# A state-space scan with a gated feed-forward on one core: pairs 3 to 11 turned by one transposing DMA a pair, all wide decays in one prologue set, and SP's and GpSimd's work for pairs 2 to 6 reordered

## The chip, the core and the metric

The kernel runs on one NeuronCore of a Trainium2 chip. The core has a matrix engine (TensorE, PE in the profile), a vector engine (VectorE, DVE), a scalar engine (ScalarE, ACT), GpSimd (POOL), a queue engine that only issues DMAs here (SyncE, SP), and 16 DMA engines that all queues share. The metric is the device time of one execution in microseconds; lower is better.

## The reference

For each of 4 batches and 8 heads, a scan over 768 positions in chunks, with head size 32 and state size 16, and then a feed-forward layer over the 3072 tokens (the heads side by side make 256 features):

```python
cum = np.cumsum(la, axis=-1)                      # la: log of a, in a chunk
L = np.exp(cum[..., :, None] - cum[..., None, :]) * causal
M = einsum('bhin,bhjn->bhij', Cc, Bc) * L
y = einsum('bhij,bhjd->bhid', M, xc) \
    + einsum('bhin,bhnd->bhid', Cc, state) * exp(cum)
state = exp(sum(la)) * state + sum_j(Bc x xc * exp(cum[-1] - cum))
...
out = (relu(x @ w_gate) * (x @ w_val)) @ w_out    # 256 -> 1536 -> 256
```

## The kernel before

**Tiling.** The scan works in chunks of 128 positions, two at a time: a pair is 256 tokens of one batch, three pairs a batch (PPB), twelve pairs in all (NPAIR). The feed-forward works in blocks of 512 tokens, two pairs each, six blocks (NBLK). The decay is not applied to the score matrix: B is divided by the running product of `a`, and C is multiplied by it, after which the scores need only a causal mask.

**What is done for a pair.** `load...` brings x, B and C from memory. `scale_bc` multiplies B and C by their decays and makes them bf16, with token positions on the partitions and the 8 heads x 16 states (128) along the row. `cast_x` makes x bf16. Then B and C must be turned, so that heads x states lie on the partitions: `transp`/`turn` do this with TensorE transposes into PSUM, and `tevac` copies the results out, B twice, each time with half of the heads set to zero (`BT`), and C once (`CT`). `G` forms the scores of the 8 heads: 16 products with a contraction over 32 partitions (two heads, of which one is zeroed). `gevac` brings them to bf16 with the causal mask: on VectorE by a product with `maskUT`, on ScalarE by a plain copy that GpSimd masks behind it (`causal`). `Dm` multiplies them by x, `inter` adds C times the carried state, and `yevac` copies the sum, transposed, to `yT`, which is the feed-forward's input. `astep` adds B^T x of a chunk to the state in PSUM (`A_ps`), and `sevac` copies the blocks of it that belong to one head each.

**Three layouts.** Pairs 0 to 3 (`p < NWIDE`) are loaded wide: partition p holds tokens 2p and 2p+1, so that a memory run is 128 bytes. Their B and C get their decays from small fp32 products of their own (`wide_decay`, `wide_factors`, in the sets [1] and [2, 3]), and B is sorted back to the order of the tokens for `astep` by four products with a permutation (`sort_b`, `sort_evac`). Pairs 4 and 5 are loaded with one token on a partition and turned by TensorE. For pairs 6 to 11 (`p >= NRUN`, batches 2 and 3) B and C are loaded a second time, a whole batch at once, with runs of 24 positions on a partition (`load_seq`); VectorE scans the decays in that layout (`seq_scan` to `seq_mids`), GpSimd scales (`seq_scale`), VectorE turns 32x32 blocks (`seq_turn`) and sorts and masks the words (`seq_part`). Their states come from `arun`, in `A_ps`' bank.

**The feed-forward.** `gv` makes one slice of 128 hidden features for 512 tokens, `gvp` two slices for 256 tokens; ScalarE takes the relu (L715, L742), VectorE the product (L719, L749). `outs` makes 128 output rows.

**Order.** Every engine's instructions run in the order in which the program is written (`in_order`). The order is laid out by hand at the end of the kernel (L830 to L1008) and from block 2 on by a loop (L1010): the feed-forward of a block, with `scale` of the next pairs in between, then `section(P, Q)`, which finishes pair P and forms the scores of Q, then `outs`. PSUM has one bank for `A_ps` and seven (`bank`) that are used in turn. DMAs of the loads and most stores are issued by SP in the order of the program, the weights by GpSimd.

Of the kernel before, what the change touches and what calls it, by code (L numbers as in the profile page):

```python
# [8 lines left out]
FP32 = mybir.dt.float32  # L9
# [20 lines left out]
def kernel(  # L30
# [41 lines left out]
    NWIDE = 4  # L72
# [25 lines left out]
    def load(p, q):  # L98
        b, c0 = p // PPB, 2 * (p % PPB)
        if p >= NRUN:  # L100
            xr = raw.tile([128, 2, NH, D], FP32, tag="xr", name="xr")
            br = raw.tile([128, 2, NH, N], FP32, tag="br", name="br")
            for i in range(2):
                sl = slice((c0 + i) * 128, (c0 + i + 1) * 128)
                q.dma_start(out=xr[:, i], in_=x[b, :, sl, :].rearrange("h s d -> s h d"))
                q.dma_start(out=br[:, i], in_=B[b, :, sl, :].rearrange("h s n -> s h n"))
            st[p] = {"xr": xr, "br": br}
            return
        xr = raw.tile([128, 2, NH, D], FP32, tag="xr", name="xr")
        bcr = raw.tile([128, 2, 2, NH, N], FP32, tag="bcr", name="bcr")  # L110
        for i in range(2):
            sl = slice((c0 + i) * 128, (c0 + i + 1) * 128)
            q.dma_start(out=xr[:, i], in_=x[b, :, sl, :].rearrange("h s d -> s h d"))
            for src, j in ((B, 0), (C, 1)):
                q.dma_start(out=bcr[:, i, j],
                            in_=src[b, :, sl, :].rearrange("h s n -> s h n"))
        st[p] = {"xr": xr, "bcr": bcr}

    U = S // 32
    B0 = NRUN // PPB  # L120
    NSEG = 2 * (NB - B0)
    seq = {}

    def load_seq(b, q):

        s = {}
        for src, k in ((B, "B"), (C, "C")):
            r = raw.tile([128, 2, U, N], FP32, tag="seq" + k, name="seq" + k, bufs=2)
            q.dma_start(
                out=r.rearrange("p t u n -> p t (u n)"),  # L130
                in_=src[b].rearrange("(t q) (j u) n -> (q j) t (u n)", t=2, u=U))
            s[k] = r
        seq[b] = s
# [32 lines left out]
    smasks = const.tile([128, 2, 2, 128], BF16)  # L166
    pick = const.tile([2 * BH, 2, BH], FP32)
    pairs = identf.rearrange("p (h w) -> p w h", w=2)
    nc.vector.tensor_copy(pick[:, 1], pairs[:, 1])
    sel = const.tile([2 * BH, 128], FP32)  # L170
# [51 lines left out]
    def wide_decay(ps, d=None):  # L222

        if d is None:
            d = bank("wdec", (128, len(ps), 2, 8))
        first = True
        for k, p in enumerate(ps):
            b, c0 = p // PPB, 2 * (p % PPB)
            for i in range(2):
                w, o = (c0 + i) // HC, ((c0 + i) % HC) * 128  # L230
                for r in range(2):
                    nc.tensor.matmul(  # L232
                        out=d[64 * i:64 * i + 64, k, r],
                        lhsT=cp[:, o + r:o + 128:2], rhs=pick[:, w, 8 * b:8 * b + 8],
                        start=first or (k == 0 and r == 0), stop=True,
                        tile_position=(0, 64 * i), skip_group_check=True)
                first = False
        return d
# [27 lines left out]
    def wide_factors(ps, d):  # L266
        f = const.tile([128, len(ps), 2, 2, 8], FP32, name="wf%d" % ps[0])
        nc.vector.reciprocal(f[:, :, 0], d)
        nc.vector.tensor_copy(f[:, :, 1], d)
        for k, p in enumerate(ps):  # L270
            factors[p] = f[:, k].rearrange("p j r h -> p (j r) h")

    scaleBC = glob.tile([128, NB, NC, 2, 8], FP32)
# [12 lines left out]
    def decay_evac(d):  # L286
        for w in range(2):
            cs = slice(w * HC, (w + 1) * HC)
            nc.scalar.copy(
                out=scaleBC[:, :, cs, 1, :].rearrange("p b k h -> p k b h"), in_=d[:, :, w])  # L290

    def inverse(b, c0, c1):
        nc.vector.reciprocal(scaleBC[:, b, c0:c1, 0, :], scaleBC[:, b, c0:c1, 1, :])

    ah = const.tile([128, NSEG, U], FP32)
    a0 = const.tile([128, NSEG, U], FP32)
    hd = const.tile([128, 2, NSEG, U], FP32)
    tot = const.tile([128, 32], FP32)
    tott = const.tile([128, 32], FP32)
    lead = const.tile([128, 2, 17], FP32)  # L300
    half = const.tile([128, 1], FP32)
    mids = const.tile([128, 32], FP32)
    pre = const.tile([128, 32], FP32)

    def load_a(q):
        q.dma_start(out=ah, in_=a[B0:NB].rearrange("b (t q) (j u) -> (q j) (b t) u", t=2, u=U))

    def seq_start():
        for v in (a0, tot, lead):
            nc.gpsimd.memset(v, 0.0 if v is a0 else 1.0)  # L310
        nc.gpsimd.memset(smasks, 0.0)
        nc.gpsimd.tensor_copy(a0[:, :, 0], ah[:, :, 0])
        nc.gpsimd.memset(ah[:, :, 0], 0.0)

    def seq_masks():
        nc.gpsimd.tensor_scalar_mul(words, tmask, -1.0)
        for q in range(4):
            r = slice(32 * q, 32 * q + 32)
            for v in range(2):
                nc.gpsimd.tensor_copy(  # L320
                    smasks[r, v, :, 32 * q:32 * q + 32],
                    tmask[r].unsqueeze(2).to_broadcast([32, 2, 32]))

    def seq_scan():
        local = hd[:, 1]
        nc.vector.tensor_tensor_scan(
            out=local.rearrange("p k u -> p (k u)"), data0=ah.rearrange("p k u -> p (k u)"),
            data1=a0.rearrange("p k u -> p (k u)"), initial=0.0, op0=ALU.mult, op1=ALU.add)

    def seq_totals():  # L330
        nc.vector.tensor_copy(tot[:, 0:NSEG], hd[:, 1, :, U - 1])
        nc.vector.transpose(out=tott, in_=tot)

    def seq_lead():
        for k in range(2):
            nc.vector.tensor_tensor_scan(
                out=lead[:, k, 1:17], data0=tott[:, 16 * k:16 * k + 16],
                data1=zero.to_broadcast([128, 16]), initial=1.0, op0=ALU.mult, op1=ALU.add)
        nc.vector.reciprocal(half, lead[:, 0, 16:17])

    def seq_mids():
        nc.vector.tensor_scalar_mul(mids[:, 0:16], lead[:, 0, 0:16], half)
        nc.vector.tensor_copy(mids[:, 16:32], lead[:, 1, 0:16])
        nc.vector.transpose(out=pre, in_=mids)

    def seq_decay():
        local = hd[:, 1]
        nc.gpsimd.tensor_tensor(
            out=local, in0=local, in1=pre[:, 0:NSEG].unsqueeze(2).to_broadcast([128, NSEG, U]),
            op=ALU.mult)  # L350

    def seq_inverse(b):
        r = slice(2 * (b - B0), 2 * (b - B0) + 2)
        nc.vector.reciprocal(hd[:, 0, r], hd[:, 1, r])

    U32 = mybir.dt.uint32
    V = U // 2
# [130 lines left out]
    def tevac(p, beng, ceng):  # L488
# [20 lines left out]
        if not wide:  # L509
            c_copy()  # L510
# [564 lines left out]
```

## Time and profile before

| | us |
|---|---|
| median of 3 runs (lowest, highest) | 125.64 (125.1, 126.44) |
| the profiled execution | 124.8 |
| its span, first to last instruction | 123.0 |
| TensorE busy | 118.3 |
| VectorE busy | 92.1 |
| ScalarE busy | 74.6 |
| GpSimd busy | 49.7 |

In the rows of the timeline, the first column is the start from the beginning of the span, the second how long the instruction or the run of equal instructions lasted, then the engine, the line, the operation, what it writes and reads, the shapes and the count. In brackets stands how long the engine was idle before it and what ended that. A name with q (SPq) is an engine's queue, for DMA issues. In the row of a wait the numbers are the total, the number of times and the longest. A "group" row gives the busy time of all its instructions and the mean of one in ns. How long a DMA takes from its issue to its landing is given as lowest, median and highest.

### The profile page before, as it was taken

Reading aid. Unit: us, or ns where it says so; the run is one execution under the profiler, and the core shown is the slowest. Engines: PE = TensorE matmul, PEld = TensorE weight load, DVE = VectorE, ACT = ScalarE, POOL = GpSimd, SP = SyncE. Lnnn points to the kernel's source line nnn. Section 1 sums busy time; section 2 is a strip of 40 time slices with the busy share of each in tenths; the row PEclk is TensorE's granted clock in tenths of the full one; section 3 lists DMA queues with packets and bytes.
Section 4 is the critical chain, followed back from the end, with each engine's and each line's share of the span. In section 5 each row is a group of like instructions: output and inputs, shape, how many; then the busy total and the mean of one; then the engine's idle time right before and its main releaser. Section 6 shows DMA issues by size and latency. Waiting matters only on the chain.

```text
span 123.0 us, 3313 instructions
## 1 busy us (share of the span) xinstructions
PE 118.3 (96%) x1251; PEld 81.1 (66%) x1257; DVE 92.1 (75%) x196; ACT 74.6 (61%) x148; POOL 49.7 (40%) x102
## 2 busy tenths in 40 slices
PE   6999999999999999999999999999999999999990
PEld 4678795578888989744478644588544587444780
DVE  2786898889999859879995889981898770678420
ACT  4376668888764461767663776746676644767310
POOL 7989741885745676477330640030700030000000
PEclk9999999999999999999999999999999999999999
DMA  2999999999989979969921282003200003100022
GB/s 61 201 193 209 168 167 190 130 102 174 162 101 278 140 137 191 199 201 211 132 24 62 83 137 22 5 0 106 70 3 0 0 5 128 43 0 0 0 91 85
DMA packets 63568, 12.95 MB, mean 105 GB/s; under 512 B 55168, under 2 KB 63552, under 8 KB 63552
## 3 DMA queue, kind: packets, MB, share of 16 engines
q1 hardware_dynamic: 54160, 9.47, 42.9%
q0 software_dynamic: 4272, 2.36, 14.6%
q10 hardware_dynamic: 5120, 0.90, 3.9%
q8 instruction: 10, 0.16, 0.5%
q14 instruction: 6, 0.05, 0.1%
HBM read 11.94 MB, written 3.15 MB: 123 GB/s over the span
## 4 chain that ended last, share of the span: by engine, by line
PE 95%; DVE 1%; issue 0%; ACTq 0%; ACT 0%; DVEq 0%
PE o L760 25%; PE val L707 20%; PE gate L704 18%; PE gate L734 7%; PE val L734 6%; PE w L189 4%; PE y L670 3%; PE g L544 3%; PE y L660 2%; PE A_ps L586 1%; PE tp L486 1%; PE wdec L232 1%; PE dec L279 1%; PE o L796 1%; PE bp L463 1%; PE fdec L247 0%
## 5 line engine op out<-in xcount | busy, mean ns | idle before, releaser
L719 DVE TENSOR_TENSOR h<-r,val 128x512 bf16<-128x512 bf16 x54 | 35.9, 685 | 10.2 <-ACT r L715 9.6
L715 ACT ACTIVATE r<-gate 128x512 bf16<-128x512 f32 x54 | 32.2, 598 | 12.2 <-PE gate L704 11.7
L707 PE MATMUL val<-yT,wv 128*128 128x512 bf16 x108 | 32.1, 379 | 0.3
L760 PE MATMUL o<-wo,h 128*128 128x256 bf16 x276 | 32.3, 273 | 0.0
L704 PE MATMUL gate<-yT,wg 128*128 128x512 bf16 x102 | 30.8, 379 | 0.0
L552 POOL TENSOR_SCALAR_AFFINE_SELECT gs<-gs 128x512 bf16<-128x512 bf16 (+1 forms) x26 | 13.6, 547 | 41.6 <-ACT gs L569 41.6
L760 PEld LDWEIGHTS <-h 128*128 128x128 bf16 x276 | 26.2, 98 | 4.0
L576 DVE TENSOR_TENSOR gs<-g,maskUT 128x512 bf16<-128x512 f32 (+1 forms) x32 | 17.6, 601 | 7.1 <-PE g L544 4.0
L707 PEld LDWEIGHTS <-wv 128*128 128x128 bf16 x108 | 10.6, 98 | 12.7
L704 PEld LDWEIGHTS <-wg 128*128 128x128 bf16 x108 | 10.4, 98 | 11.1
L569 ACT CAST gs<-g 128x512 bf16<-128x512 f32 (+1 forms) x26 | 11.8, 512 | 2.9 <-PE g L544 2.9
L742 ACT ACTIVATE r<-gate 128x512 bf16<-128x512 f32 x18 | 10.6, 604 | 2.7 <-PE gate L734 2.3
L749 DVE TENSOR_TENSOR h<-r,val 128x512 bf16<-128x512 bf16 x18 | 11.8, 678 | 0.3 <-ACT r L742 0.2
L734 PE MATMUL gate<-yT,wg 128*128 128x256 bf16 x72 | 10.8, 273 | 0.0
L734 PE MATMUL val<-yT,wv 128*128 128x256 bf16 x72 | 10.8, 273 | 0.0
L779 ACT COPY ob<-o 128x512 f32<-128x512 f32 x6 | 3.5, 586 | 8.6 <-PE o L760 8.6
L774 ACT COPY ob<-o 128x256 f32<-128x256 f32 x10 | 3.7, 373 | 7.3 <-PE o L760 6.8
L734 PEld LDWEIGHTS <-wv 128*128 128x128 bf16 x72 | 7.0, 98 | 0.9
L692 ACT CAST yT<-y 128x512 bf16<-128x512 f32 x10 | 5.9, 586 | 2.4 <-PE y L670 2.3
L734 PEld LDWEIGHTS <-wg 128*128 128x128 bf16 x72 | 6.7, 98 | 0.9
L189 PE MATMUL w<-warm 128*128 128x256 bf16 x27 | 5.9, 380 | 1.2 <-DVE tmask L159 1.2
L452 POOL CAST xb<-xr 128x512 bf16<-128x512 f32 x10 | 6.1, 612 | 1.0 <-DMA xr<-in_x_dram 1.0
(124 smaller groups left out, 123.2 us busy)
## 6 DMA issues: line engine op xcount, KB each, us to landing
xr<-in_x_dram SPq DMA_DIRECT2D x24, 128.0 KB, 3.7
out_dram<-ob SPq DMA_DIRECT2D x6, 256.0 KB, 2.6
out_dram<-ob SPq DMA_DIRECT2D x9, 128.0 KB, 1.8
wo<-in_moe_w_out_dram POOLq DMA_DIRECT2D x1, 768.0 KB, 8.9
seqB<-in_B_dram SPq DMA_DIRECT2D x2, 384.0 KB, 3.7
seqC<-in_C_dram SPq DMA_DIRECT2D x2, 384.0 KB, 4.2
br<-in_B_dram SPq DMA_DIRECT2D x12, 64.0 KB, 3.2
wg<-in_moe_w_gate_dram POOLq DMA_DIRECT2D x3, 128.0 KB, 4.3
```

The lines of the kernel that those rows point to most:

```text
L189: nc.tensor.matmul(out=w[:, 0:cols], lhsT=warm[:, 0:128], rhs=warm[:, 0:cols], start=True, stop=True)
L552: nc.gpsimd.affine_select(out=dst, in_=dst, pattern=[[0, n], [1, 128]], compare_op=ALU.is_ge, fill=0.0, base=0, channel_multiplier=-1)
L569: nc.scalar.copy(out=d[:, q, h], in_=g[q][:, h])
L576: nc.vector.tensor_tensor(out=d[:, q, h], in0=g[q][:, h], in1=m[:, h], op=ALU.mult)
L704: nc.tensor.matmul(out=g, lhsT=wg[:, k, fs], rhs=yT[:, k, tk], start=(k == 0), stop=(k == 1))
L707: nc.tensor.matmul(out=v, lhsT=wv[:, k, fs], rhs=yT[:, k, tk], start=(k == 0), stop=(k == 1))
L715: nc.scalar.activation(r, g, AF.Relu)
L719: nc.vector.tensor_tensor(out=fst[b][:, f], in0=r, in1=v, op=ALU.mult)
L734: nc.tensor.matmul(out=o[:, j], lhsT=w[:, k, fs], rhs=yT[:, k, tk], start=(k == 0), stop=(k == 1), skip_group_check=True)
L742: nc.scalar.activation(r, g, AF.Relu)
L749: nc.vector.tensor_tensor(out=fst[b][:, f:f + 2, u * 256:(u + 1) * 256], in0=r, in1=v, op=ALU.mult)
L760: nc.tensor.matmul(out=o[:, ts % 2], lhsT=fst[b][:, f, ts * 128:(ts + 1) * 128], rhs=wo[:, f], start=(f == 0), stop=(f == NF - 1), skip_gr ...
```

## The change

NWIDE is 3 instead of 4. The layouts of pairs 3, of pairs 4 and 5, and of pairs 6 to 11 give way to one:

- `load_bc` loads C wide (two tokens a partition) and B narrow (one).
- `scale_bc` writes into one of four bf16 tiles `pads` of 128 x 6 x 128: for each of the two chunks, B's even and odd heads into two blocks whose other columns stay zero (`diag`), and C into the last two. From pair 6 on it writes B, dense, a second time (`bt`), for `arun`.
- `dturn` turns all six blocks with one transposing DMA from SP, from SBUF to SBUF.
- `G` and `inter` read the result as it lies; the scores' columns then stand with even tokens first, so that the masks (`maskW`, and `causal` with a wide pattern), the y bank and `yevac` follow that order. `astep` for pairs 3 to 5 becomes two products of 128 columns, one for the even heads and one for the odd.
- `wide_decay` makes the decays of all pairs in one set, in the prologue, where five warming products and the set [1] stood; C of all pairs reads its copy `wD`. The decays of single tokens (`decay`) are now for B alone (`cN`, and `iN`, their inverse).
- The functions `load_seq` and all `seq_...` go, with their masks.
- In the hand-written part the loads, scalings, casts and turns of pairs 2 to 6 are put in another order.

```diff
-    NWIDE = 4
+    NWIDE = 3
...
+    def load_bc(p, q=nc.sync, hold=False):
...
+        q.dma_start(out=cr.rearrange("p h r n -> p h (r n)"),
+                    in_=C[b, :, sl, :].rearrange("h (p r) n -> p h (r n)", r=2))
         for i in range(2):
             sl = slice((c0 + i) * 128, (c0 + i + 1) * 128)
+            q.dma_start(out=br[:, i], in_=B[b, :, sl, :].rearrange("h s n -> s h n"))
+    def load(p):
+        load_bc(p)
+        load_x(p)
...
+    pads = [glob.tile([128, 6, 128], BF16, name="pad%d" % k) for k in range(NPAD)]
+    for k in range(2, 4):
+        nc.vector.memset(pads[k][:, 0:4], 0.0)
...
+    def wide_decay():
+        d = bank("wdec", (128, PPB, 2, BH))
+        for c in range(0, NC, 2):
+            for r in range(2):
+                for i in range(2):
+                    w, o = (c + i) // HC, ((c + i) % HC) * 128
                     nc.tensor.matmul(
+                        out=d[64 * i:64 * i + 64, c // 2, r],
+                        lhsT=cp[:, o + r:o + 128:2], rhs=pick[:, w],
...
+        if p >= NWIDE:
+            s["pad"] = t = pads[p % NPAD]
+            for i in range(2):
                 eng.tensor_tensor(
+                    out=diag(t, 2 * i), in0=s["br"][:, i].rearrange("s (q t) n -> s q t n", t=2),
+                    in1=iN[:, i, p].rearrange("s (q t) -> s q t", t=2).to_broadcast(
+                        [128, 4, 2, N]), op=ALU.mult)
+            eng.tensor_tensor(
+                out=t[:, 4:6].rearrange("s r (h n) -> s r h n", n=N),
+                in0=s["cr"].rearrange("s h r n -> s r h n"),
+                in1=wD[:, p % PPB, :, 8 * b:8 * b + 8].to_broadcast([128, 2, NH, N]), op=ALU.mult)
+            if p >= NRUN:
+                bt = att.tile([128, 2, 128], BF16, tag="bt", name="bt")
...
+    def dturn(p):
+        s = st[p]
+        s["TT"] = att.tile([128, 6, 128], BF16, tag="TT", name="TT")
+        nc.sync.dma_start_transpose(out=s["TT"], in_=s["pad"].rearrange("s k m -> s (k m)"))
...
+            for t in range(2):
+                nc.tensor.matmul(
+                    out=heads[:, :, t], lhsT=st[p]["pad"][:, 2 * i + t], rhs=own[:, :, t],
+                    start=(c == 0 and t == 0), stop=(c == NC - 2), skip_group_check=True)
...
     astep(0, 0)
-    keep_warm(5)
-    d1 = wide_decay([1])
-    wide_factors([1], d1)
+    dw = wide_decay()
+    wide_factors(dw)
     load_wide(2, nc.sync, True)
-    load_x(2)
     sevac(0, 0)
     scale_bc(1, nc.gpsimd)
     dall = decay()
-    decay_evac(dall)
+    nc.scalar.copy(out=wD, in_=dw)
     split_y(0)
+    decay_evac(dall, 0)
+    load_x(2)
+    load_bc(3)
...
     astep(1, 1)
-    d2 = wide_decay([2, 3], later)
-    wide_factors([2, 3], d2)
     gvp_mul(*u4)
-    load_wide(3, nc.sync, True)
+    inverse(NWIDE, 6)
+    scale_bc(2, nc.gpsimd)
     load_x(3)
-    load(4, nc.sync)
-    load(5, nc.sync)
-    load_seq(2, nc.sync)
-    load(6, nc.sync)
-    scale(2, nc.gpsimd, nc.gpsimd)
+    cast_x(2, nc.gpsimd)
+    for k in range(2):
+        nc.gpsimd.memset(pads[k][:, 0:4], 0.0)
+    scale_bc(3, nc.gpsimd)
+    dturn(3)
+    load_bc(4)
+    load_bc(5)
     sevac(1, 1)
...
-    turn(3, True)
-    sort_b(3, False)
-    tevac(3, nc.vector, nc.scalar)
     gvp(1, 0, 0)
...
     gvp_evac(*u)
-    seq_masks()
-    scale(4, nc.gpsimd, nc.gpsimd)
+    scale_bc(4, nc.gpsimd)
+    dturn(4)
+    load_x(4)
+    load_x(5)
+    load_bc(6)
+    cast_x(4, nc.gpsimd)
     gvp(1, 0, 6)
...
     scale(5, nc.gpsimd, nc.gpsimd)
-    turn(4)
-    tevac(4, nc.vector, nc.scalar)
+    dturn(5)
+    load_x(6)
     gvp(1, 1, 10)
     outs(0, 0)
     state(4, 0)
     Gs(4)
+    scale_bc(6, nc.gpsimd)
     outs(0, 1)
     state(4, 1)
+    dturn(6)
+    load(7)
     outs(0, 2)
-    turn(5)
-    tevac(5, nc.vector, nc.scalar)
     outs(0, 3)
-    load(8, nc.sync)
+    load(8)
     section(4, 5)
-    scale(6, nc.gpsimd, nc.gpsimd)
+    cast_x(6, nc.gpsimd)
...
     for b in range(2, NBLK):
+        if more:
+            scale(Q, nc.gpsimd, nc.gpsimd)
+        if P + 3 < NPAIR:
+            load(P + 3)
+        if more:
+            dturn(Q)
...
             if f == 4 and R < NPAIR:
                 scale(R, nc.gpsimd, nc.gpsimd)
+                dturn(R)
```

More of the change, by code (lines that the diff above doesn't have):

```diff
@@ L284, in decay @@
         return d
[L286 to L357, printed above, removed]
-    packs = [glob.tile([128, V, 32, 2], BF16, name="pack%d" % k) for k in range(4)]
-    words = const.tile([128, 2], mybir.dt.int32)
@@ L569, in gevac @@
             nc.scalar.copy(out=d[:, q, h], in_=g[q][:, h])
-            causal(d[:, q, h], 2 * n)
+            causal(d[:, q, h], 2 * n, p >= NWIDE)
         for q in range(3, -1, -1):
@@ L835 @@
     first_scale(0, fB, bs0[:, 0:2])
+    load_x(1, True)
     first_scale(1, dC, bs0[:, 2:4])
@@ L896 @@
     gvp_mul(*u0)
-    later = bank("wdec", (128, 2, 2, 8))
     u2 = gvp(0, 0, 2, False)
```

288 lines of the change are left out of this document (98 added, 190 removed).

## The prediction

> **What bounds the kernel now.** I read the busy shares and the chain of waits first, then TensorE's own waits, then the timeline of TensorE against those of GpSimd, SP and ScalarE around pairs 1 to 6.
>
> ```profile
> span 123.0 us, 3313 instructions
> ## 1 busy us (share of the span) xinstructions
> PE 118.3 (96%) x1251; PEld 81.1 (66%) x1257; DVE 92.1 (75%) x196; ACT 74.6 (61%) x148; POOL 49.7 (40%) x102
> ```
>
> ```profile
> PE 95%; DVE 1%; issue 0%; ACTq 0%; ACT 0%; DVEq 0%
> ```
>
> ```profile
> PE w L189 <- DVE tmask L159: 1.2, 1, 1.2
> ```
>
> The chain that ends last is TensorE for 95% of the span, and TensorE's only recorded wait is the 1.2 us before its first warming matmul. From there it goes from one product to the next. So what the change takes from VectorE (the 32x32 turns and word masks of pairs 6 to 11, the masked copies of the turned B of pairs 3 to 5) gains nothing by itself. Only two things move the end: matmuls taken out of TensorE's queue, and operands that now arrive too late for it. I work out both in turn. The profiled execution took 124.8 us, 1.8 over its span, and that 1.8 stays. The median of the runs shown is 125.64, 0.84 above it.
>
> **What leaves TensorE.** Pair 3 loses its four transposes and the four products that sort its B:
>
> ```profile
> 25.41 0.27 PE L486 MATMUL tp<-ident,bs 128*128 128x128 bf16 x2
> 25.53 0.28 PE L486 MATMUL tpc<-ident,bs 128*128 128x128 bf16 x2
> 25.64 0.39 PE L463 MATMUL bp<-bs,order 128*128 128x128 bf16 x4
> 25.86 0.60 PE L734 MATMUL gate<-yT,wg 128*128 128x256 bf16 x4
> ```
>
> From the start of the first to the start of the gate product is 25.86 - 25.41 = 0.45 us. (The second column is longer, because matmuls overlap; I go by starts throughout.) Pairs 4 and 5 lose four transposes each:
>
> ```profile
> 36.79 0.39 PE L486 MATMUL tp<-ident,bs 128*128 128x128 bf16 x4
> 37.01 0.60 PE L734 MATMUL gate<-yT,wg 128*128 128x256 bf16 x4
> ```
>
> ```profile
> 42.48 0.39 PE L486 MATMUL tp<-ident,bs 128*128 128x128 bf16 x4
> 42.70 1.47 PE L760 MATMUL o<-wo,h 128*128 128x256 bf16 x12
> ```
>
> That is 0.22 twice, 0.44. The wide decays of pairs 2 and 3 go from behind pair 1 into the prologue:
>
> ```profile
> 15.13 0.27 PE L586 MATMUL A_ps<-xb,bx 128*128 128x256 bf16 x1
> 15.33 0.68 PE L232 MATMUL wdec<-pick,cp 64*64 64x8 f32 x16
> 15.94 0.61 PE L734 MATMUL gate<-yT,wg 128*128 128x256 bf16 x4
> ```
>
> ```profile
> 15.33 0.37 ACT L651 CAST yT<-y 128x256 bf16<-128x256 f32 x1 [0.27 <-PE y L646]
> ```
>
> The 0.61 us from 15.33 to 15.94 cannot all be had. The gate product behind it reads the yT half that ScalarE is still copying until 15.33 + 0.37 = 15.70. Today the decays hide that copy; without them it ends last. With about 0.05 to hand over, the product starts at 15.75, so I credit 0.19 of the 0.61.
>
> The prologue pays for it:
>
> ```profile
> 7.70 0.71 PE L189 MATMUL w<-warm 128*128 128x256 bf16 x5
> 8.34 0.42 PE L232 MATMUL wdec<-pick,cp 64*64 64x8 f32 x8
> 8.69 0.88 PE L279 MATMUL dec<-pick,cp 64*128 64x64 f32 x6
> 9.50 0.41 PE L670 MATMUL y<-gs,xb 128*32 128x128 bf16 x16
> ```
>
> Five warming matmuls and eight fp32 passes lasted 8.69 - 7.70 = 0.99. In their place come 12 fp32 products, 24 passes, of the same 64 stationary columns with 32 moving columns instead of 8. At 0.35/8 = 0.044 a pass they take 1.05, so decay() slips by about 0.1. No row has 32 moving columns. The bounds are the 16 passes at 0.61/16 = 0.038, which gives 0.91 and a gain of 0.1, and decay()'s own passes at 0.81/6 = 0.135 with 128 stationary and 64 moving columns, which gives 3.2 and a loss of 2.2. I take the near row, because the stationary size is the same: a cost of 0.1.
>
> The outer products that build the state of pairs 3 to 5 (five of 256 columns) become ten of 128, against the block-placed B. The four sorting products above cost 0.22/4 = 0.055 each at 128 columns, so ten make 0.55; the old form took at most 39.40 - 39.20 = 0.20 each (rows below) with its hand-over. I set this to nothing, with 0.5 either way. The scores, the intra-chunk products and the state products of pairs 6 to 11 keep their number and size; only the order of their columns differs.
>
> Sum: 0.45 + 0.44 + 0.19 - 0.10 = 0.98, about 1.0 us. If nothing comes late, the profiled execution becomes 123.8, and the median 125.64 - 1.0 = 124.6.
>
> **What can now come late.** The operands of G() for pairs 3 to 6 come over a chain: loads on SP, two block-placing multiplies and one for C on GpSimd (a further one from pair 6 on), the transposing DMA on SP, and in between x loads on the same SP queue and casts on the same GpSimd queue. The times at which TensorE asks for them:
>
> ```profile
> 24.20 0.41 PE L670 MATMUL y<-gs,xb 128*32 128x128 bf16 x16
> ...
> 27.70 0.40 PE L544 MATMUL g<-CT,BT 32*128 32x128 bf16 x16
> ...
> 39.20 0.27 PE L586 MATMUL A_ps<-xb,bs 128*128 128x256 bf16 x1
> 39.40 0.40 PE L544 MATMUL g<-CT,BT 32*128 32x128 bf16 x16
> ...
> 44.67 0.40 PE L544 MATMUL g<-CT,BT 32*128 32x128 bf16 x16
> ...
> 49.74 0.40 PE L544 MATMUL g<-CTs,BM 32*128 32x128 bf16 x16
> ```
>
> Less the savings ahead of each, G(3) is due at 27.16, state(4) at 38.44, G(4) at 38.64, G(5) at 43.69, G(6) at 48.76. GpSimd, and SP's loads:
>
> ```profile
> 2.21 0.52 POOL L180 MEMSET order<- 128x512 bf16 x1
> ...
> 21.98 1.58 POOL L552 TENSOR_SCALAR_AFFINE_SELECT gs<-gs 128x512 bf16<-128x512 bf16 x3 [2.13 <-ACT gs L569]
> ...
> 33.39 1.06 POOL L433 TENSOR_TENSOR bs<-bcr,scaleBC 128x512 bf16<-128x512 f32 x1 [0.71 <-DMA bcr<-in_C_dram]
> 34.40 0.60 POOL L452 CAST xb<-xr 128x512 bf16<-128x512 f32 x1
> ...
> 46.89 0.76 POOL L419 TENSOR_TENSOR bt<-br,scaleBC 128x128 bf16<-128x128 f32 x2
> ```
>
> ```profile
> 11.89 3.34 SPq L95 DMA_DIRECT2D xr<-in_x_dram  x2
> ```
>
> ```profile
> DMA to landing us min/median/max: 2.8/3.7/7.6
> ```
>
> A multiply of 128 elements a partition is 0.40 (two in 0.76 overlap a little), one of 512 is 1.06; C's 256 lie between, about 0.62. Pair 3's scaling thus takes 0.8 + 0.62 = 1.4 where one multiply took 1.06. SP is free of pair 2's x at 15.23. Three loads for pair 3 at about 0.7 are issued by 17.4 and land by the median of the last row (the x loads' time from issue to landing, 3.7) at 21.1. Until then GpSimd zeroes two pads (0.52 each) in time that it now spends waiting. So pair 3's pad is ready near 22.6.
>
> Two things hang on that. The causal masks of pair 2 now stand behind this scaling in GpSimd's queue and start at 22.6 instead of 21.98. The first of three is done 1.58/3 = 0.53 later, at 23.1, and the intra-chunk products of pair 2 (24.20, now 24.1) read it: an idle 1 us covers it, and is used up if pair 3's loads land after 22. And pair 3's transposing DMA starts at 22.6 with 27.16 - 22.6 = 4.5 us to land.
>
> No transposing DMA is in the trace. It moves 128 x 768 bf16, 192 KB, in one instruction. From below I bound it by the quickest landing of an x load (128 KB), 2.8, and from above by the slowest, 7.6. I take 4.0, a little over the median, because it carries half as much again. SP is held for each of the two x loads above for 3.34/2 = 1.7 us; I take 1.5 for a transposing DMA.
>
> VectorE: DVE Perf Modes of the Trainium skill (section "The three transpose paths") gives 1309 ns for a 128x128 block by DMA against 390 ns on TensorE, and advises TensorE where PSUM will do; six blocks one after another would be an estimated 7.9 us. Advanced Engine Details and Errata of the Trainium skill ("X-Bar Transpose") says instead that such DMAs are as fast as ordinary ones. No run shown so far decides between them; by the first the sum is that of the late-landing case below, by the second the one above.
>
> Pair 4: in the trace its scaling starts at 33.39, after 0.71 of waiting for data that shared the DMA engines with w_out. Its loads now stand ahead of three x loads that used to come first; They can land between 22.6 + 1.5 + 3 x 0.7 + 3.7 = 29.9, unhindered, and 33.4, as now; I take 30.5, since less stands ahead of them. Scaled by 31.9, turned by 35.9, due 38.64: 2.7 spare. But its x loads now stand behind the turn on SP: 31.9 + 1.5 + 0.6 + 3.7 = 37.7, cast (0.60) by 38.3, due 38.44: nothing spare. Pair 5's scaling follows that cast: 38.3 + 1.4 + 4.0 = 43.7, due 43.69: nothing spare. Pair 6's scaling, 2.05 with the fourth multiply, follows pair 4's masks, which end at about 38.64 + 0.40 + 0.86 (the copies below) + 2 x 0.53 = 41.0: 41.0 + 2.05 + 4.0 = 47.05, due 48.76: 1.7 spare.
>
> ```profile
> 39.88 0.86 ACT L569 CAST gs<-g 128x512 bf16<-128x512 f32 x2 [1.64 <-PE g L544]
> ```
>
> From pair 7 on a turn is issued most of a block of gate and value products, or three output tiles, ahead, and isn't at risk.
>
> ScalarE's copies of y for pairs 3 to 11 now write every other column. It has 39% idle, so a slower copy would be hidden; I give it nothing.
>
> **The rivals.** First, slower: the turns land late. A landing of L us stalls G(3) by L - 4.5, G(5) by L - 4.0 and G(6) by L - 5.7, and these add, since each turn's scaling stands on GpSimd behind masks or casts that wait for the pair before. At L = 5 that is 1.5 and more than eats the gain (126.1); at 6 it is 1.5 + 2.0 + 0.3 = 3.8, so 128.4; at 7.6 it is 3.1 + 3.6 + 1.9 = 8.6, so 133.2. It decides from L = 4.75, where both stalls together make 1.0. For it: the turn queues behind loads on the same SP queue, and the slowest x load took 7.6. Against it: the loads that were issued early for batch 2 are gone from this stretch. Chance 0.30.
>
> Second, the x loads behind a waiting turn: if SP is held by the turn for 4 us instead of 1.5, state(4) stalls by 2.4 and the net is +1.4, so 127.0. Chance 0.10.
>
> Third, better: the credits I cut are had in full. 0.45 + 0.44 + 0.61, and 0.1 in the prologue, make 1.6: 124.0. For it speaks that TensorE never waits; against it the copy that ends at 15.70. Chance 0.18.
>
> **How the numbers follow.** The likeliest case, 0.42, is that every operand is in time or late by tenths: 124.6, between 124.2 and 125.2 with the outer products' bound. A change of 1% (1.26 us) is about what a measurement of this kernel can tell from none. Faster than 124.38: 0.15 of the third rival and 0.10 of the main case, 0.25. Slower than 126.9: 0.26 of the first and 0.08 of the second, 0.34. The rest, 0.41, is within 1%. The range goes from 123.2 (the third rival with a quiet run) to 128.4 (L = 6); beyond it lie half of the first rival and a little below, under 0.2.
>
> **What would show it.** Right: the step from the last gv of pair 2's block to gvp(1,0,0) shorter by 0.45, and TensorE's list of waits still nearly empty. Wrong: waits of G() or of the state products on a DMA or on xb around pairs 3 to 6; a landing of the transposing DMA over 4.75 us; wide decays at more than 0.05 a pass; masks of pair 2 that start after 23.5.

## The result, and the profile after

The changed kernel takes 130.58 us, median of 5 runs (129.61 to 130.81); the kernel before, run beside it, takes 125.51 (5 runs, 124.61 to 126.44). The ratio is 1.040, 95% interval 1.033 to 1.047: 4% slower, where 124.6 with a range to 128.4 was forecast. In the ratios, here and below, a kernel's runs that took over 1.5% longer than its fastest are left out. The profiled execution took 130.74 with a span of 129.0, so 6.0 us more span than before.

First the page of the changed kernel: span, busy times, the row of the granted clock and the row of bytes moved (40 slices of 3.2 us), and the chain that ended last, by engine.

```profile
span 129.0 us, 3245 instructions
...
PE 119.0 (92%) x1235; PEld 80.8 (63%) x1241; DVE 82.0 (64%) x161; ACT 74.3 (58%) x145; POOL 49.2 (38%) x98
...
PEclk9999999967999999999999999999999999999999
...
GB/s 64 204 198 209 201 170 122 15 115 175 162 84 153 121 189 116 122 175 243 118 153 129 167 46 124 157 5 0 122 86 26 0 0 83 85 0 0 0 81 81
...
PE 72%; DMA 13%; SPq 5%; DVE 3%; POOL 2%; ACT 2%; issue 1%; ACTq 0%
```

VectorE gave up 10 us of work, as the change intends, and TensorE carries 72% of the chain instead of 95%. Its longest waits, and the rows of its timeline that have one behind the prologue:

```profile
PE g L429 <- DMA TT<-pad: 2.6, 2, 1.4
PE y L571 <- POOL gs L440: 1.6, 2, 1.2
PE w L176 <- DVE tmask L140: 1.2, 1, 1.2
PE gate L638 <- ACT yT L596: 0.5, 1, 0.5
PE gate L638 <- ACT yT L552: 0.4, 1, 0.4
```

```profile
15.64 0.60 PE L638 MATMUL gate<-yT,wg 128*128 128x256 bf16 x4 [0.35 <-ACT yT L552]
25.20 0.23 PE L571 MATMUL y<-gs,xb 128*32 128x128 bf16 x2 [1.25 <-POOL gs L440]
25.79 0.60 PE L571 MATMUL y<-gs,xb 128*32 128x128 bf16 x14 [0.36 <-POOL gs L440]
26.56 0.38 PE L608 MATMUL gate<-yT,wg 128*128 128x512 bf16 x1 [0.16 <-issue]
...
35.24 0.49 PE L638 MATMUL gate<-yT,wg 128*128 128x256 bf16 x3 [0.51 <-ACT yT L596]
67.03 0.40 PE L429 MATMUL g<-TT 32*128 32x128 bf16 x16 [1.24 <-DMA TT<-pad]
73.50 0.40 PE L429 MATMUL g<-TT 32*128 32x128 bf16 x16 [1.35 <-DMA TT<-pad]
```

The starts of the scores, G(4) to G(8), show where the 6.0 us arise (all from the timeline of TensorE; the columns e3, e5 and e9 are experiments told below):

| start of | before | after | e3 | e5 | e9 |
|---|---|---|---|---|---|
| G(4) | 39.40 | 42.76 | 41.91 | 40.48 | 39.22 |
| G(6) | 49.74 | 52.88 | 52.03 | 50.59 | 50.42 |
| G(7) | 62.41 | 67.03 | 64.70 | 63.27 | 63.10 |
| G(8) | 67.45 | 73.50 | 69.75 | 68.31 | 68.14 |
| span | 123.0 | 129.0 | 125.3 | 123.8 | 123.7 |

Up to G(4) 3.36 are lost; from there to G(6) 0.22 are won back; the steps to G(7) and G(8) are 1.48 and 1.43 longer; behind G(8) nothing more changes (6.05 there, 6.0 at the end). So there are two places, and both lead to what SP issues. (Turn 3 is the transposing DMA of pair 3, x(4) are the x loads of pair 4, and w_out is the 768 KB of output weights that GpSimd issues in one DMA.) Its queue in the changed kernel (start, time in which SP was held, what it issued):

```profile
13.86 2.44 SPq L105 DMA_DIRECT2D cr<-in_C_dram  x1
16.34 3.21 SPq L109 DMA_DIRECT2D br<-in_B_dram  x2
19.59 1.30 SPq L95 DMA_DIRECT2D xr<-in_x_dram  x2
24.59 1.32 SPq L333 DMA_TRANSPOSE TT<-pad  x1
25.96 0.57 SPq L105 DMA_DIRECT2D cr<-in_C_dram  x1
26.57 1.52 SPq L109 DMA_DIRECT2D br<-in_B_dram  x2
28.13 3.90 SPq L105 DMA_DIRECT2D cr<-in_C_dram  x1
32.08 2.95 SPq L109 DMA_DIRECT2D br<-in_B_dram  x2
36.17 1.33 SPq L333 DMA_TRANSPOSE TT<-pad  x1
37.55 2.81 SPq L95 DMA_DIRECT2D xr<-in_x_dram  x4
...
59.87 0.43 SPq L105 DMA_DIRECT2D cr<-in_C_dram  x1
60.35 1.55 SPq L109 DMA_DIRECT2D br<-in_B_dram  x2
61.94 1.50 SPq L95 DMA_DIRECT2D xr<-in_x_dram  x2
63.55 1.34 SPq L333 DMA_TRANSPOSE TT<-pad  x1
```

And GpSimd's timeline, around the masks of pair 2 (24.52), the issue of w_out (26.06), the end of pair 4's scaling, the cast of x(4) (41.59), and the last write of pair 7's pad:

```profile
20.89 0.40 POOL L306 TENSOR_TENSOR pad<-br,iN 128x128 bf16<-128x128 f32 x1 [1.63 <-DMA br<-in_B_dram]
23.59 0.40 POOL L306 TENSOR_TENSOR pad<-br,iN 128x128 bf16<-128x128 f32 x1 [2.29 <-DMA br<-in_B_dram]
...
24.52 1.59 POOL L440 TENSOR_SCALAR_AFFINE_SELECT gs<-gs 128x512 bf16<-128x512 bf16 x3
26.06 1.08 POOL L193 DMA_DIRECT2D wo<-in_moe_w_out_dram  x1
...
35.17 0.40 POOL L306 TENSOR_TENSOR pad<-br,iN 128x128 bf16<-128x128 f32 x1 [0.67 <-DMA br<-in_B_dram]
35.53 0.62 POOL L310 TENSOR_TENSOR pad<-cr,wD 128x256 bf16<-128x256 f32 x1
41.59 0.61 POOL L358 CAST xb<-xr 128x512 bf16<-128x512 f32 x1 [5.44 <-DMA xr<-in_x_dram]
...
55.94 0.62 POOL L310 TENSOR_TENSOR pad<-cr,wD 128x256 bf16<-128x256 f32 x1
```

Three things are to be read. From 20.9 to 24.6 SP stands before turn 3, whose pad isn't written; in the slice around that (the eighth) 15 GB/s are moved. Then all that pair 4 needs is issued one behind the other, with w_out's 768 KB in flight beside it. Two things hold turn 4 back: SP is held in the loads for pair 5 from 28.13 to 35.03, and pair 4's own second load of B, issued before 28.1, is scaled only at 35.17, so that the pad is complete at 36.15 (35.53 + 0.62). (In the view of the tile br these two loads took 7.4 and 7.9 us from issue to landing, where the median of the page is 3.2.) The pad comes last: turn 4 leaves at 36.17, x(4) behind it at 37.55, and its cast starts at 41.59 after 5.44 of waiting. Finally, pair 7's pad is complete by 56.56, but turn 7 leaves only at 63.55, behind stores and the five loads of pair 9. The turns themselves are quick; the view of the tile TT (duration of the issue on SP in ns, lowest, median, highest; and from issue to landing in us):

```profile
L333 SPq DMA_TRANSPOSE TT<-pad x9: 1215/1336/1968, 24.6 to 94.8; - x9
...
DMA to landing us min/median/max: 2.8/3.4/4.6
```

One thing looks like a cause and is none. After the waits at 25.20 and 25.79 the clock was halved for some 4 us (the digits 6 and 7 of PEclk): from the gate product at 26.56 to G(3) at 30.72 pass 4.16 us, where e3 needs 2.5. But state(4), which started at 42.55, could not start before the cast of x(4) ended at 42.20, and four more runs of the changed kernel had a mean clock of 0.999 to 1.0 and took 129.61 to 130.81 all the same. The slow products filled what would for the most part have been a wait.

### The profile page after: what moved, and what is told of

Its sections match the earlier page's. It is cut to its first block, busy times and chain, and to the rows that moved or that the text cites. A ratio compares the mean times of both kernels' runs of the same rounds, so it can differ in the third digit from the quotient of the medians.

```text
span 129.0 us, 3245 instructions
## 1 busy us (share of the span) xinstructions
PE 119.0 (92%) x1235; PEld 80.8 (63%) x1241; DVE 82.0 (64%) x161; ACT 74.3 (58%) x145; POOL 49.2 (38%) x98
## 4 chain that ended last, share of the span: by engine, by line
PE 72%; DMA 13%; SPq 5%; DVE 3%; POOL 2%; ACT 2%; issue 1%; ACTq 0%
PE o L664 20%; PE val L611 16%; PE gate L608 15%; DMA TT<-pad 6%; DMA br<-in_B_dram 5%; PE gate L638 5%; PE val L638 5%; PE w L176 3%; PE g L429 2%; SPq L95 2%; PE y L571 2%; SPq L105 2%; DMA out_dram<-ob 1%; POOL gs L440 1%; PE y L561 1%
## 5 line engine op out<-in xcount | busy, mean ns | idle before, releaser
L623 DVE TENSOR_TENSOR h<-r,val 128x512 bf16<-128x512 bf16 x54 | 36.4, 686 | 16.7 <-ACT r L619 15.6
L619 ACT ACTIVATE r<-gate 128x512 bf16<-128x512 f32 x54 | 31.8, 599 | 11.1 <-PE gate L608 10.6
L464 DVE TENSOR_TENSOR gs<-g,maskW 128x512 bf16<-128x512 f32 (+1 forms) x26 | 14.1, 592 | 15.7 <-issue 13.4
L611 PEld LDWEIGHTS <-wv 128*128 128x128 bf16 x108 | 10.6, 98 | 12.9 <-issue 0.3
L653 DVE TENSOR_TENSOR h<-r,val 128x512 bf16<-128x512 bf16 x18 | 11.8, 680 | 3.5 <-PE val L638 1.9
L638 PE MATMUL gate<-yT,wg 128*128 128x256 bf16 x72 | 11.9, 289 | 0.9 <-ACT yT L596 0.5
L638 PE MATMUL val<-yT,wv 128*128 128x256 bf16 x72 | 11.6, 286 | 0.0
L596 ACT CAST yT<-y 128x512 bf16<-128x512 f32 x10 | 7.2, 718 | 4.6 <-PE y L571 4.5
L306 POOL TENSOR_TENSOR pad<-br,iN 128x128 bf16<-128x128 f32 x18 | 6.9, 401 | 5.6 <-DMA br<-in_B_dram 5.6
L638 PEld LDWEIGHTS <-wv 128*128 128x128 bf16 x72 | 7.5, 104 | 1.2
```

The source lines that it names most:

```text
L464: nc.vector.tensor_tensor(out=d[:, q, h], in0=g[q][:, h], in1=m[:, h], op=ALU.mult)
L596: eng.copy(out=dst, in_=src)
L611: nc.tensor.matmul(out=v, lhsT=wv[:, k, fs], rhs=yT[:, k, tk], start=(k == 0), stop=(k == 1))
L619: nc.scalar.activation(r, g, AF.Relu)
L623: nc.vector.tensor_tensor(out=fst[b][:, f], in0=r, in1=v, op=ALU.mult)
L638: nc.tensor.matmul(out=o[:, j], lhsT=w[:, k, fs], rhs=yT[:, k, tk], start=(k == 0), stop=(k == 1), skip_group_check=True)
```

## The experiments

Twelve kernels; edits are to the changed kernel unless said otherwise. Times are medians of all runs of a kernel, ratios are to the kernel before run beside it. That one took 124.4 to 124.7 here and 125.5 beside the changed kernel, so an edit's worth is taken from the ratios, against the changed kernel's 1.040; 0.001 is 0.12 us.

**e1: the masks ahead of pair 3's scaling.** Tests the first wait.

```diff
-    scale_bc(3, nc.gpsimd)
-    dturn(3)
-    load_bc(4)
-    load_bc(5)
     sevac(1, 1)
...
     gevac(2, 3)
+    scale_bc(3, nc.gpsimd)
+    dturn(3)
+    load_bc(4)
+    load_bc(5)
     state(2, 0)
```

> The changed kernel with the causal masks of pair 2 ahead of pair 3's scaling in GpSimd's queue (the scaling, its turn and the loads of pairs 4 and 5 are written behind gevac(2, 3)). Theory (order on GpSimd): the masks run at about 21.7 to 23.2, the intra-chunk products of pair 2 lose both their waits (1.25 and 0.36 us), and the granted clock stays at 1.00 behind them. What is won there (2.3 of stall, 1.45 of half clock) is mostly not kept: the x loads of pair 4 still stand on SP behind two turns and land at about 41, so that the state products of pair 4, then due near 38.8, wait for their cast; net gain 0.3 to 1.5 us (129.1 to 130.3), with a new wait of the pair-4 state products or G(3). Rival (the waits are independent, nothing else is near its limit): the full 3.8 us, 126.8. Rival (the transposing DMA is what is slow): no gain, and G(3) waits for it by over 2 us.

134.76 (132.88 to 136.24). The wait of pair 2's products is gone, as expected, but the kernel is slower still, and G(3) waits for its turn, as by the last rival. TensorE's timeline, SP's queue and GpSimd's in e1:

```profile
33.04 0.61 PE L429 MATMUL g<-TT 32*128 32x128 bf16 x16 [6.24 <-DMA TT<-pad]
```

```profile
24.39 1.32 SPq L333 DMA_TRANSPOSE TT<-pad  x1
...
26.59 6.52 SPq L109 DMA_DIRECT2D br<-in_B_dram  x2
```

```profile
24.30 1.08 POOL L193 DMA_DIRECT2D wo<-in_moe_w_out_dram  x1
```

Turn 3 left at nearly the same time as in the changed kernel, but 0.09 us behind w_out instead of 1.47 ahead of it, and landed after 8.6 us instead of 2.9.

**e8: e1 with w_out held back**, by a one-element VectorE write to its tile, until behind gvp(1,0,0).

```diff
-    weights_out(0, NF)
     cast_x(3, nc.gpsimd)
...
     gvp(1, 0, 0)
+    nc.vector.memset(wo[0:1, 0, 0:1], 0.0)
+    weights_out(0, NF)
```

> The kernel of e1_masks_first with w_out's load held back until the first gvp of pair 2's block (some 3 us later). Theory (in e1 the turn of pair 3 took 8.6 us to land because w_out's 768 KB were issued with it and the engines share them out): the turn lands within 3.5 us, G(3) waits 1.0 us or less instead of 6.2, the clock stays up, and the time falls by 4 to 8 us, to 127 to 130; the state products of pair 4 then wait for the cast of x(4). Rival (a transposing DMA of this size is that slow when loads of x are queued with it): G(3) still waits by over 3 us, above 131.

129.97, ratio 1.041 [1.037, 1.046]; w_out left at 27.61, turn 3 at 24.83, and G(3) waited 0.50 instead of 6.24. So it was w_out that the turn met, and not the turn that is slow. The time is the changed kernel's all the same: state(4) still waits 1.75 for x(4), and G(8) 1.38 for its turn. Pair 4's pad was complete at 32.0 here, 4 us sooner, but SP was held in pair 5's loads until 33.9 and then 3.22 by turn 4 itself, so that x(4) left at 37.25, hardly sooner than in the changed kernel.

**e3: turns ahead of loads in the loop.** `dturn(Q)` goes ahead of `load(P + 3)`, and `load(P + 4)` behind `dturn(R)`.

```diff
             scale(Q, nc.gpsimd, nc.gpsimd)
+            dturn(Q)
         if P + 3 < NPAIR:
             load(P + 3)
-        if more:
-            dturn(Q)
-        if P + 4 < NPAIR:
-            load(P + 4)
...
                 dturn(R)
+                if P + 4 < NPAIR:
+                    load(P + 4)
```

> The changed kernel with the turns of the loop issued ahead of the loads: dturn(Q) before load(P + 3), and load(P + 4) behind dturn(R). Theory (the turns of pairs 7 and 8 are late because they queue on SP behind five loads each): G(7) and G(8) lose their waits of 1.24 and 1.35 us, 128.0. Rival (they are late because the transposing DMA itself lands late in a busy stretch): G(7) and G(8) still wait by 0.7 us or more each, 129.5 to 130.6.

126.42 (124.89 to 127.17), ratio 1.012 [1.008, 1.017]: the largest single part, 0.028 or some 3.5 us. In the table 2.90 of it lie between G(6) and G(8); the 0.85 ahead of G(4) lie where the edit changes nothing. Turn 7 leaves at 59.12 instead of 63.55, and the waits of G(7) and G(8) are gone. TensorE's longest remaining wait (total, times, longest):

```profile
PE A_ps L479 <- POOL xb L358: 1.2, 1, 1.2
```

With the clock at 1.0 in this profile, the wait for x(4) shows, which the slow products hid in the changed kernel.

**e5: e3, and x(4) ahead of the loads for pair 5.**

```diff
     load_bc(4)
+    load_x(4)
     load_bc(5)
...
     dturn(4)
-    load_x(4)
```

> The kernel of e3_turn_first with the x loads of pair 4 issued ahead of the loads of pair 5, instead of behind them and the turn of pair 4. Theory (what binds up to 42 us is SP's queue: pair 4's x stands behind the loads of pair 5, which w_out's load holds up, and a turn): the wait of pair 4's state products for their cast (1.2 us in e3) goes; 0.8 to 1.2 us less than e3, 125.2 to 125.6. Rival (the DMA engines are full anyway, so that only the order of landing changes): G(4) or G(5) waits for its turn instead, and the time stays within 0.4 of e3's 126.4.

125.36 (10 runs, 123.95 to 126.18), ratio 1.002 [0.999, 1.006]. The wait for x(4) is gone and G(4) starts 1.43 earlier than in e3. Two moves in SP's order thus take back 0.038 of the 0.040. What stays is the masks' wait (1.02 and 0.36 here), 0.51 for the copy of y and 0.35 for the other one.

**e6: e3, and pair 4's B and C ahead of turn 3**, to fill the stretch in which SP stands.

```diff
-    dturn(3)
     load_bc(4)
+    dturn(3)
```

> The kernel of e3_turn_first with pair 4's loads of B and C issued ahead of the turn of pair 3, in the 3 us in which SP stands waiting for pair 3's pad and the DMA engines are nearly idle. Theory (the head of SP's queue, a turn that waits for GpSimd, keeps loads back that nothing else holds): pair 4's B lands near 26 instead of 34.8, its scaling starts right behind pair 3's masks (31.3), its turn and its x follow 2 to 3 us earlier, and the state products' wait goes; 125.2 to 125.6, as in e5. G(3) may come up to 1 us later, since its turn now has fresh loads ahead of it. Rival (the engines are the limit): pair 3's turn lands so much later that G(3) waits by over 1.5 us, 126.4 or more.

126.96 (4 runs, 125.73 to 132.86), ratio 1.014 [1.008, 1.020]: no gain over e3. The profiled execution was the longest, 132.86. There turn 3 left at 24.79, 0.10 behind w_out, and landed after 9.1: e1's case again. A turn that leaves 0.1 us behind w_out, and not 1.5 ahead of it as in the changed kernel and e3, lands some 6 us later.

**e4: the copy of y in two.** ScalarE's strided copy (0.72 us each, against 0.59 before; L596, mean 718 ns and L692, 586 ns) is written as two of 256 columns.

```diff
+        elif eng is nc.scalar and p >= NWIDE:
+            for k in range(2):
+                eng.copy(out=dst[:, k], in_=src[:, k])
```

> The changed kernel with ScalarE's copy of y for pairs 3 to 11 as two copies, one for each half of the features. Theory (the wait of gvp(1, 0, 10) on yT is a dependency on the whole stretch of memory between the two halves of the strided copy, which holds columns that the copy doesn't write): the wait of 0.5 us at 34.6 goes, because each half is a stretch of its own; ScalarE pays about 0.2 more for a pair, hidden; 130.0. Rival (it is a true dependency or a bank of PSUM): the wait stays or grows, 130.6 to 130.9.

128.53 (128.14 to 128.75), ratio 1.033 [1.031, 1.036]. The wait of 0.51 is gone, and the ratio is 0.007 or 0.8 us lower, but the changed kernel's own interval begins at 1.033: that the time follows is likely, not shown.

**e2: twelve warming products ahead of pair 2's products**, against the clock's fall at 26 us.

```diff
     inter(2, 1)
+    keep_warm(12)
     Dm(2)
```

> The changed kernel with 12 warming products (about 1.3 us) in the wait ahead of the intra-chunk products of pair 2; the wait itself stays. Theory (the clock gate fell because TensorE stood idle for 1.6 us): the products from 26.5 to 30.7 run at 0.11 us per 256 columns instead of 0.21, granted clock 1.00 there, G(3) comes 1.4 us earlier; part of it may be given back at the pair-4 state products, which wait for x(4)'s cast. Rival (those products are slow because w_out's load or the pad writes disturb the reading of SBUF): they stay at 0.21 and the time stays at 130.6.

129.26 (127.42 to 130.32), ratio 1.030 [1.024, 1.036]. The late fall of the clock is gone. But that 0.010, or 1.2 us, were won is not shown: the ratio rests on the two shorter of four runs (127.42 and 128.7), and the others took 129.81 and 130.32 at nearly full clock (0.997 and 0.995). The trace, of the run of 129.81, then waits for turns (1.8 in three places), for x(4) (0.7) and for a store's buffer (1.0).

**e7: all of it mended.** e3, the copy for pair 3 in two, the masks first, pair 4's B and C, x(4) and turn 4 ahead of w_out and of pair 5's loads, and gvp(1, 0, 4) ahead of G(3).

```diff
     gevac(2, 3)
+    scale_bc(3, nc.gpsimd)
+    dturn(3)
+    load_x(4)
     state(2, 0)
...
     cast_x(3, nc.gpsimd)
+    scale_bc(4, nc.gpsimd)
+    dturn(4)
+    load_bc(5)
+    load_x(5)
+    load_bc(6)
+    weights_out(0, NF)
```

> All mends together, on the changed kernel: turns ahead of loads in the loop, masks of pair 2 ahead of pair 3's scaling, pair 4's B and C ahead of pair 3's turn and its x behind it, pair 4 scaled and turned before w_out's load is issued, gvp(1, 0, 4) ahead of G(3), and pair 3's copy of y in two halves. Theory (the change takes 1.2 us out of TensorE's queue, and all the loss is order on SP and GpSimd): TensorE's waits fall to the 0.35 for yT and some tenths, and the time to 0.990 to 0.997 of the kernel before, 123.2 to 124.0. Rival (nine turns and 11,000 more packets cannot be fitted beside the loads): a wait of over 1 us for a turn, a cast or w_out remains, 125 to 127.

125.95, but in two groups: six runs at 123.39 to 125.19 with a clock of 0.997 to 1.0, six at 126.71 to 127.94 with 0.983 to 0.986. The ratio of the first group is 0.996 [0.991, 1.000]. In the profile, which is of the second group, the clock stands at a half from 10 to 13 us, in the prologue. The change had taken five warming products out there.

**e10: the kernel before without these five products.** The clean test of that.

```diff
-    keep_warm(5)
     d1 = wide_decay([1])
```

> The kernel before, with nothing changed but that the five warming products ahead of its first set of wide decays are left out. Theory A: some of the runs show a mean clock of 0.986 or less and are 1.5 to 3 us longer than 124.6, where none of the 32 runs of the kernel before so far had a clock under 0.996; the others lie at 124.0 to 124.7. Theory B: all the clocks stay at 0.996 or more, and the time is 124.0 to 124.7 in every run.

126.16: four of six runs at 126.03 to 126.47 with a clock of 0.986, two at 124.31 and 125.27 with 0.995 and 1.0; none of 67 runs of the kernel before in these comparisons lay under 0.996. Windows of 1 us, first of the kernel before, then of e10 (length, then busy time and count of TensorE, its weight loads, VectorE, ScalarE and GpSimd, the granted clock, DMA share, GB/s):

```profile
11.00:12.00 1.00, 1.00 (x14) 0.91 (x11) 0.55 (x3) 0.98 (x3) 1.00 (x2) 1.00 1.43 207
```

```profile
9.00:10.00 1.00, 0.78 (x20) 0.47 (x19) 0.73 (x5) 0.38 (x2) 1.00 (x3) 1.00 1.43 195
10.00:11.00 1.00, 1.00 (x7) 0.75 (x7) 0.56 (x2) 0.37 (x1) 1.00 (x2) 0.57 1.50 199
11.00:12.00 1.00, 1.00 (x8) 0.83 (x7) 0.36 (x1) 0.38 (x2) 1.00 (x2) 0.50 1.42 209
```

Theory A holds for the kernel before: the five products look like filler, 0.7 us that nobody waits for, and without them the clock fell in four of six runs.

**e9: e7 with the five products back**, ahead of the wide decays.

> The kernel with all the mends, and five warming products ahead of the wide decays, where the kernel before has them. Theory A: the half clock from about 9.7 to 13 us, which six of the twelve runs without them had (mean clock 0.986, 126.7 to 127.9 us), comes of the five missing products of 256 columns; with them every run has a clock of 0.996 or more and lies at 123.4 to 125.5, the products cost at most their 0.7 us, median 124.2. Theory B: the clock falls for another reason (the fp32 wide decays, 24 short passes that follow anyway); then a third to a half of the runs still show 0.986 or less and 126.7 or more, and the median stays at about 125.9.

125.42 (124.89 to 127.51), ratio 1.006 [1.004, 1.008], the clock at 1.0 in all six runs. Theory A is right on the clock and wrong on the time by 1.2 us: the mended kernel isn't below the kernel before. (Two of the six runs took 127.24 and 127.51.) In the trace G(4) starts at 39.22, 0.18 ahead of the kernel before, and G(5) then waits 1.02 for turn 5, which SP issues at 40.71 behind pair 6's loads. The five products take 8.26 - 7.62 = 0.64 us of TensorE again:

```profile
7.62 0.71 PE L176 MATMUL w<-warm 128*128 128x256 bf16 x5
8.26 0.91 PE L216 MATMUL wdec<-pick,cp 64*64 64x32 f32 x24
```

**e11: e9 with pair 6's B and C behind turn 5.**

```diff
     load_x(5)
-    load_bc(6)
...
     dturn(5)
+    load_bc(6)
```

> e9_all_rewarmed with pair 6's loads of B and C put behind pair 5's turn in SP's queue. In e9's trace that turn left at 40.71, behind three loads that took 2.4 us, though its pad was written by 39.57, and landed at 45.3, 1.02 us late for G(5). Theory: the turn leaves at about 39.6 and lands by 44.0, G(5) waits at most 0.2, and the time falls by about 1.0, to 124.3 (ratio to the kernel before 0.995 to 1.000). Rival: what makes the turn late is the load of pair 5 beside w_out's transfer, so that the pad is later in other runs and the median stays at 125.2 to 125.5; or G(6) inherits the wait, which the trace would show as a wait for TT at 49 to 51 us.

127.18 (126.97 to 130.49), ratio 1.024 [1.019, 1.028]: not faster but slower. The trace is of the longest run (130.49, clock 0.987), and shows the place that the rival named: SP was held in pair 5's loads of B from 29.82 to 38.16 (5.94 us in e9), turn 5 left at 41.52, and G(5) and G(6) waited 0.38 each; gv behind them waits 2.33 for an output buffer as well. Why the other runs, too, are longer than e9's is not shown.

**e12: e9 with pair 5's B and C ahead of x(4) and turn 4.**

```diff
     dturn(3)
+    load_bc(5)
     load_x(4)
...
     dturn(4)
-    load_bc(5)
```

> e9_all_rewarmed with pair 5's loads of B and C issued right behind pair 3's turn, ahead of x(4) and of pair 4's turn. In e9 they leave from 28.95 on, behind the issue of w_out's 768 KB (27.46), and SP is held in them to 35.8; in e11 to 38.2, and the turns of pairs 5 and 6 are late. Theory: it is the meeting with w_out that holds them; issued from about 26.4 they hold SP for 2 to 4 us, pad 5 is written well ahead of 38, turn 5 leaves by 39 and G(5) waits at most 0.2; 124.3 (123.8 to 124.6 in most runs), turn 4 leaves at 29 to 31 and is in time for 39. Rival: SP is held in these loads just as long, until 33 or later, wherever they stand; then x(4) and turn 4 come after 34, state(4) or G(4) waits 0.5 to 2, and the time is 125 to 127.

125.67 (9 runs, 124.69 to 127.06), ratio 1.008 [1.005, 1.011]. SP's queue in e12:

```profile
26.69 1.20 SPq L109 DMA_DIRECT2D br<-in_B_dram  x2
...
29.66 6.34 SPq L333 DMA_TRANSPOSE TT<-pad  x1
```

The loads are now quick, and the turn that stands in their old place is held 6.34 us in their stead. What SP issues from 2.4 to 2.8 us behind w_out's issue (27.0 to 27.5 in e9, e11 and e12) is held until 35.8 to 38.2. The theory had the meeting right and its effect on G(5), 0.56 of waiting, wrong. No order tried is shown to be faster than the kernel before; e7 with the clock up comes level with it.

## Why the prediction was wrong, step by step

**Right in kind: what leaves TensorE, though the five products had to come back.** 0.98 was forecast, all of it ahead of G(5). In e9, at full clock and without its wait of 1.02, G(5) would start at 44.33, which is 37.27 behind G(0) at 7.06; in the kernel before it was 44.67 - 7.25 = 37.42. That is 0.15 less with the five products in it; without their 0.64 it would be 0.79. So the forecast's sum was nearly right, but most of it is the time of the five products, without which the clock falls in many runs (e7, e10). gvp(0,1,0) waits 0.35 for the copy of yT that was to end last, and starts at 15.64, 0.30 ahead of before. The 24 decay passes took 8.65 - 7.81 = 0.84, that is 0.035 each, taken at 0.044:

```profile
7.81 0.91 PE L216 MATMUL wdec<-pick,cp 64*64 64x32 f32 x24
8.65 0.88 PE L266 MATMUL dec<-pick,cp 64*128 64x64 f32 x6
```

**Right: the turn's own time.** 3.4 us median, 2.8 to 4.6, where 4.0 was taken, and SP held for 1.34 (1.5 taken). The first rival's condition, a landing over 4.75, did not arise in the changed kernel; it did where a turn met w_out (8.6 and 9.1). The estimate of 7.9 us, six times the figure of VectorE: DVE Perf Modes of the Trainium skill ("The three transpose paths"), does not hold for six blocks in one instruction. Advanced Engine Details and Errata of the Trainium skill ("X-Bar Transpose") says that such a DMA is as fast as an ordinary one. The trace agrees: the x loads took as long (DMA issues on the page of the changed kernel; count, size where it has one, median us to landing):

```profile
xr<-in_x_dram SPq DMA_DIRECT2D x24, 128.0 KB, 3.4
...
TT<-pad SPq DMA_TRANSPOSE x9, 3.4
```

**Failed: pair 3's loads, "Three loads for pair 3 at about 0.7 are issued by 17.4".** No row stood behind the 0.7; the quoted row of the x loads said 1.7 each. They took 2.44 and 3.21 (two), were issued by 19.55 instead of 17.4, and the last landed just ahead of 23.59, where its scaling starts, instead of at 21.1. The masks started at 24.52 instead of 22.6. The step named its own limit (loads that land after 22) and was past it. It cost 1.6 us of waiting, which in the changed kernel the later wait for x(4) covered (e8, without it, takes as long), and which stands open in e5.

**Failed: pair 4, "I take 30.5", and with it "its x loads now stand behind the turn on SP: 31.9 + 1.5 + 0.6 + 3.7".** Pair 4's B was to land at 30.5, at the latest at 33.4. Its second load could be scaled only at 35.17; the pad was complete at 36.15 instead of 31.9, and turn 4 left at 36.17. From there the sum held: the cast of x(4) started 5.42 later, at 41.59, where 5.8 was forecast. So state(4)'s operand came at 42.2 instead of 38.3, 3.9 over. The sum also left out the three loads of `load_bc(5)` that the diff puts ahead of turn 4. They held SP until 35.03, so that a pad at 31.9 would have gained little; e8 shows just that (pad at 32.0, turn 4 at 33.98, x(4) at 37.25). The timeline of the kernel before has such a hold already, 2.6 us behind the issue of its w_out (24.53):

```profile
27.14 4.16 SPq L115 DMA_DIRECT2D bcr<-in_B_dram  x1
```

The second rival had the place right; it priced SP's hold at 4 us of a waiting turn and gave 127.0 a chance of 0.10. e5 removes the wait of state(4) by one move, x(4) ahead of pair 5's loads and of turn 4, so that the place of x(4) is shown as its cause; pair 4's pad is as late there (35.7).

**Failed: "From pair 7 on a turn is issued most of a block of gate and value products, or three output tiles, ahead, and isn't at risk."** It counted the turn's place in the program, and did not count what the loop puts ahead of it on SP. Turn 7 left 7.0 us after its pad was ready, and G(7) and G(8) waited 2.6 us together. e3 takes that away and is worth 0.028 of the 0.040; 2.9 of its some 3.5 us lie at these two places.

**Not considered: the clock, and the copy of y.** The five products were counted as time, and not as what holds the clock. e10 shows the other use, though the changed kernel's own profile has full clock there, so that this is not what made it slow. The strided copy, to which the prediction gives "nothing", costs one wait of 0.51, which goes when the copy is in two (e4).

**Still open.** The five products' own 0.64 is a part of the 1.2 by which e9 lies above what was expected of it; the rest, why it spreads to 127.5 at full clock, and why SP is held beside w_out are open: the runs show where, not why.

## What to carry to other kernels

When a change puts waiting instructions on a queue that also issues loads, list that queue in program order for every stage, with the time that each issue holds it in the busiest row of the trace, and work out each due time along that list. A turn that is quick by itself was late here because of what stood ahead of it. Small products that no one waits for may be holding the clock: leave them out in an experiment of their own before counting their time as gained. A big transfer on another queue is part of the order too: a turn issued 0.1 us behind it landed some 6 us later than one issued 1.5 us ahead of it.

## What was unexpected of the hardware

A turn of 192 KB issued 0.1 us behind a 768 KB transfer from GpSimd's queue landed after 8.6 and 9.1 us (e1, e6), against 2.9 when issued 1.5 us ahead of it; turn 4, issued 0.2 to 0.9 us behind it in e7, e9 and e11, landed after 7.7 to 10.6. SP's issues, which take 0.4 to 0.6 us at their quickest (59.87 and 25.96 in the changed kernel), were held up to 6.3 us for one instruction beside the same transfer (e12).

The clock fell to a half without a long idle: in e7 with TensorE busy throughout the two microseconds in which the fall began (8 to 10), in e10 after 0.22 us of idle in the microsecond before, in the changed kernel after 1.6 us in two pieces. TensorE: Matmul & The Clock Gate of the Trainium skill ("Why this matters for your kernels") warns of gaps over about 3 us; the drops here followed shorter ones.
